# Turning keys and queries of all half batches on TensorE instead of by transposing loads

## The chip, the cores and the metric

The kernel runs on one core of a Trainium2 chip. The metric is the device time of one execution in microseconds (us); the median of three runs of the kernel before is 398.96 us (396.92 to 400.0). A core has five engines that work side by side, each through its own queue in program order: TensorE (PE in the profile; PEld is its loading of weights), VectorE (DVE), ScalarE (ACT), GpSimd (POOL) and SyncE (SP). In this kernel SP and POOL also issue the DMA transfers. TensorE writes to PSUM, a small memory of eight banks, from which DVE or ACT copy results into SBUF.

## What is computed

Attention with a sliding window and a few global tokens, then an MLP whose activation is h * cos(h):

```python
# q, k, v: (8 batches, 8 heads, 576 tokens, 64)    global_idx: 8 tokens
scores = scale * np.matmul(q, k.transpose(0, 1, 3, 2))
mask = np.abs(pos[:, None] - pos[None, :]) <= 32
mask = mask | is_global[:, None] | is_global[None, :]
attn = softmax(np.where(mask, scores, -1e9))
attn_out = np.matmul(attn, v)
x = attn_out.transpose(0, 2, 1, 3).reshape(4608, 512)
h = x @ w_in                    # (512, 2048)
out = (h * np.cos(h)) @ w_out   # (2048, 512)
```

Inputs and output are fp32; the kernel computes in fp16 with fp32 sums.

## The kernel before

**Tiles.** The work of attention is cut into 32 pairs of heads (`pr`, four to a batch) and two pairs make a half batch (`s`, 16 of them). A pair's 576 queries are cut into 11 blocks of 56; each block has, with the 8 global tokens, 64 query columns for each of the two heads, and 120 keys of the window with the 8 global keys as 128 rows. So a pair needs keys with the head dimension on partitions (`kw`, 128 x 11 x 128) and queries likewise (`qb`, 128 x 11 x 2 x 64), four buffers of each.

**How keys and queries get turned.** There are two ways in the kernel, and the constant `HY` parts them (lines 410 to 430):

- Half batches below HY = 4: `load_qk` (L256) brings k and q straight from the input into SBUF as fp16, with tokens on partitions, by two DMAs of POOL's queue. `turned` (L401) transposes a pair on TensorE: 8 rows x 2 heads = 16 transposes for keys (86 x 64 each) and 16 for queries (78 x 64) into a PSUM tile `t`. For keys ACT copies `t` into `kw` (L414); for queries ACT copies the first head and DVE the second into `qb` (L427).
- Half batches from 4 on: `cast_half` (L244) has POOL's queue cast k and q into an fp16 scratch in DRAM (`k16`, `q16`, L253), `turn_half` (L263) has SP's queue bring them back with two transposing loads into `kT` and `qT` (L265, L266), and DVE copies from there into `kw` (L417) and `qb` (L430).

Values of every half batch are cast to a scratch `v16` (L249) and loaded from there by SP's queue as overlapping windows (`load_v`, L296; the rows of the global tokens by `load_vg`, L314).

**One pair.** `scores` (L432): 11 matmuls in three groups into PSUM tiles `st`, the exponential on ACT (L442), the product with the mask on DVE (L443). `values` (L446): 22 matmuls into `pv`, then on DVE the sums and the division (L457 to L463). `turn_x` (L467): six transposes into `tx`, copied by DVE into `xT`; after a batch's last pair POOL copies its global rows (L483).

**The MLP.** `mlp_in` (one block: four matmuls of 128x512 at L491, the cosine on ACT at L494, the product on DVE at L495) and `mlp_out` (one block: four matmuls at L505; after four blocks a copy of `o` by ACT or DVE and a store by SP's queue).

**The order.** It is written out by hand and each engine keeps it. Strings give the order: `FRONT` for the first pairs, `THIRD` for s=2, and `ORDER` for each step s=3 to 15 of the loop at L684. In a step, `sa` and `sz` are the scores of the half's two pairs (three groups each), `pa` and `pz` the values, `xa` and `xz` the turns of x, `n` a sum of squares on ACT, `1` a block of `mlp_in`, `2` a block of `mlp_out` (in the early steps fewer are let through, `outs_by`), `G` the issue of casts (`casts`, L660), and `kc qc kd qd` the preparation of keys and queries of the two pairs of the next half:

```python
ORDER = "sa0 sa1 sa2 2 2 2 sz0 2 sz1 sz2 pa 1 1 2 xa pz G 1 1 2 xz n 1 1 2 kc qc 1 kd qd 2 1"
```

At the end of step s come `turn_half(s + 2)` and the value loads of half s + 2, all on SP's queue, which also holds the stores of the output. After the loop a tail does what is left of the MLP.

**PSUM.** The tiles `st`, `tx` and (after FRONT) `t` share three slots with the tag "s"; `ph` of `mlp_in` has two with the tag "h", `po` one with the tag "o", and `pv` its own.

Of the kernel before, what the change touches and what calls it, by code (L numbers as in the profile page):

```python
# [24 lines left out]
W = 120  # L25
BP = 6
KL = 32
HY = 4
RW = 8
KPAD = 4  # L30
KP = KPAD + S // RW + 10
# [23 lines left out]
def dview(ap, offset, *dims):  # L55

    return bass.AP(ap.tensor, ap.offset + offset, [list(d) for d in dims])
# [134 lines left out]
def kernel(  # L192
# [51 lines left out]
    def cast_half(s, which):  # L244

        base = s * 4 * S * D
        for x in which:
            if x == "v":
                nc.gpsimd.dma_start(v16[s * 4 * S : (s + 1) * 4 * S].rearrange("(n r) d -> n (r d)", r=16),  # L249
                                    dview(v, base, (16 * D, 4 * S // 16), (1, 16 * D)))  # L250
            else:
                src, dst = {"k": (k, k16), "q": (q, q16)}[x]
                nc.gpsimd.dma_start(dst[s].rearrange("t (h d) -> t h d", h=4),  # L253
                                    dview(src, base, (D, S), (S * D, 4), (1, D)))

    def load_qk(s):  # L256

        base = s * 4 * S * D
        for src, dst in ((k, kn[s % 2][KPAD : KPAD + S // RW]), (q, qn[s % 2][0 : S // RW])):
            nc.gpsimd.dma_start(dst.rearrange("x h r d -> x h (r d)"),  # L260
                                dview(src, base, (RW * D, S // RW), (S * D, 4), (1, RW * D)))

    def turn_half(s):  # L263

        nc.sync.dma_start(kT[s % 2][:, :, KL : KL + S], k16[s], transpose=True)  # L265
        nc.sync.dma_start(qT[s % 2][:, :, 0:S], q16[s], transpose=True)  # L266
# [19 lines left out]
    def gather(src, dst, half):  # L286
        rows = src.rearrange("b h s d -> (b h s) d")
        for h in range(2):
            nc.gpsimd.indirect_dma_start(
                out=dst[:, half, h], out_offset=None, in_=rows,  # L290
                in_offset=bass.IndirectOffsetOnAxis(ap=gidx_rows[:, 0:1], axis=0),
                element_offset=(half * 32 + h) * S * D)
# [80 lines left out]
    def build_globals(half):  # L373
        for src, dst in ((kg32, kgT), (qg32, qgT)):
            g16 = work.tile([P, P], FP16, tag="g16")
            nc.scalar.copy(g16, src[:, half].rearrange("x h d -> x (h d)"))
            t = ps.tile([P, 16 * G], FP16, tag="s", bufs=3)
            nc.tensor.transpose(t, g16, ident16)
            nc.scalar.copy(dst[:, 16 * half : 16 * half + 16], t.rearrange("x (n g) -> x n g", g=G))
        nc.scalar.copy(vg16[:, half], vg32[:, half])  # L380
# [20 lines left out]
    def turned(src, pr, n):  # L401

        t = ps.tile([P, RW, n], FP16, tag="h" if front[0] else "s", bufs=2 if front[0] else 3)
        h0 = 2 * (pr % 2)
        for r in range(RW):
            for h in range(2):
                nc.tensor.transpose(t[h * D : (h + 1) * D, r], src[:n, h0 + h, r], ident16[:n, :n])  # L407
        return t

    def local_k(pr):  # L410
        to = kw[pr % NK][:, :, G:]
        if pr < 2 * HY:
            t = turned(kn[pr // 2 % 2], pr, KP)
# [5 lines left out]
    def local_q(pr):  # L419
        if pr < 2 * HY:  # L420
            t = turned(qn[pr // 2 % 2], pr, QP)
        for h in range(2):
            hp = slice(h * D, (h + 1) * D)
            to = qb[pr % NK][hp, :, h, G:]
            if pr < 2 * HY:
                copy = nc.scalar.copy if h == 0 or pr < 2 else nc.vector.tensor_copy
                copy(view(to, (2 * C, NB), (RW, QB // RW), (1, RW)),  # L427
                     view(t[hp], (QB // RW, NB), (1, QB // RW), (QP, RW)))
            else:
                nc.vector.tensor_copy(to, view(qT[pr // 2 % 2][hp, pr % 2], (QB, NB), (1, QB)))  # L430
# [89 lines left out]
    def x_squares(s):  # L520

        sq = work.tile([P, 2 * BP * P], FP16, tag="sq", bufs=1)
        xn = xn_of.pop(s)
        nc.scalar.activation(sq, view(xn, (1, 2 * BP * P)), AF.Square,  # L524
                             accum_out=x_sq[:, s : s + 1])
# [47 lines left out]
    def one(n=1):  # L573
        for _ in range(n):

            if ins_q and ins_q[0][0] < ready[0] and ins_q[0][0] < outs_q[0][0] + 2:
                t, f = ins_q.pop(0)
                mlp_in(t, f)
                ready[1] = t * NF + f + 1

    def two(n=1):
        for _ in range(n):
            t, u = outs_q[0] if outs_q else (NTT, 0)

            need = min(t * NF + 4 * (u % 4) + 12, NTT * NF) if tail[0] else min(t * NF + 4 * (u % 4) + 7, (t + 1) * NF)
            if outs_q and need <= ready[1] and (tail[0] or NTT * NF - len(outs_q) < outs_by[0]):
                mlp_out(*outs_q.pop(0))
# [7 lines left out]
    with tc.manual_schedule():  # L595
# [48 lines left out]
        def load_values(pr):  # L644
            load_v(pr)
            load_vg(pr)
# [9 lines left out]
        def globals_kq(pr):  # L656
            globals_k(pr)
            globals_q(pr)

        def casts(s):  # L660

            nc.gpsimd.tensor_copy(gate, xn_of[s][0:1, 1, 0, 0:1])  # L662
            for n in range(4, 2 * B):
                if s == (n - 2 if n < 7 else n - 3):
                    cast_half(n, "vkq")
            if s == 4:
                for src, dst in ((k, kg32), (q, qg32), (v, vg32)):
                    gather(src, dst, 1)
# [15 lines left out]
        for s in range(2, B * NP // 2):  # L684
            if s == 2:
                nc.gpsimd.dma_start(w_out16, moe_w_out.rearrange("(c p) n -> p c n", p=P))
            outs_by[0] = 4 * (s - 2) if s < 5 else 8 * (s - 3)
            for pr in (2 * s + 2, 2 * s + 3):
                if 8 <= pr < B * NP:
                    globals_kq(pr)  # L690
            for step in (THIRD if s == 2 else ORDER).split():
                if step == "1":
                    one()
                elif step == "2":
                    two()
                elif step == "n":
                    x_squares(s - 1)
                elif step == "G":
                    casts(s)
                else:  # L700
                    f, pr = (STEPS | LOCAL)[step[0]], 2 * s + "azcd".index(step[1])
                    if pr < B * NP:
                        f(pr, *[int(x) for x in step[2:]])
            if s % 2 == 1:
                ready[0] = s // 2 + 1 + (s // 2 == B - 1)
            if s < B * NP // 2 - 2:
                turn_half(s + 2)
                load_values(2 * s + 4)
                load_values(2 * s + 5)
            if s == 5:  # L710
                build_globals(1)
# [49 lines left out]
```

## Time and profile before

| | |
|---|---|
| runs | 398.96, 400.0, 396.92 us |
| the profiled execution | span 395.4 us from the first to the last instruction; its time outside the span is not listed |
| PE busy | 328.3 us, 83% |
| DVE busy | 260.6 us, 66% |
| ACT busy | 238.8 us, 60% |
| POOL busy | 114.8 us, 29% |
| software DMA queue (POOL's) | 63952 packets, 18.75 MB, 48.4% of 16 engines |
| hardware DMA queue (SP's) | 124509 packets, 27.89 MB, 59.6% of 16 engines |
| chain that ended last | PE 67%, DMA 10%, DVE 8%, ACT 5% |
| L407 (transposes of half batches 0 to 3) | 256 instructions |
| L253 (casts of k and q, half batches 4 to 15) | 24 DMAs |
| L265, L266 (transposing loads) | 24 DMAs |

How to read it: "busy" is the sum of an engine's instructions; a matmul's listed duration holds its latency, and matmuls overlap, so PE's pace is read from the distance of their starts. In an answer of the timeline a line has start, duration, engine, line of the kernel and operation, and in brackets how long the engine had stood idle before it and what ended that. Windows give each engine's busy time in a stretch, the clock granted to TensorE (1.00 is full) and the share of the DMA engines' time that transfers took.

### The profile page before, as it was taken

The page shows a single profiled execution, that of the slowest core. Times are in us where ns is not written, and L with a number is a line of the kernel's source. Part 1 is how long each engine was busy: PE and PEld are TensorE (multiplying, and loading weights), DVE is VectorE, ACT ScalarE, POOL GpSimd, SP SyncE. Part 2 cuts the span into 40 slices and gives each one's busy share as a digit, 9 for nine tenths or more (in the row PEclk, how much of TensorE's full clock was granted, in tenths as well). Part 3 has the DMA queues.
Part 4 walks back from the last instruction along what each step waited for, and adds up shares of the span by engine and source line. Part 5 has one row for each costly group of instructions (what it writes and reads, how often), then busy time and mean ns, then how long its engine had stood idle before and what let it go on. Part 6 is the DMA issues. An engine that isn't in the chain of part 4 may idle for free.

```text
span 395.4 us, 7373 instructions
## 1 busy us (share of the span) xinstructions
PE 328.3 (83%) x2678; PEld 174.7 (44%) x2678; DVE 260.6 (66%) x600; ACT 238.8 (60%) x351; POOL 114.8 (29%) x250
## 2 busy tenths in 40 slices
PE   0272179576778889899999999999999979999993
PEld 0262164343434355455555555555555334444441
DVE  7744157555687768789788888888889354544300
ACT  1572066945575686677778678776777866244210
POOL 6573032504268275071443507223000100000000
PEclk9997558969999999999999999999999999999999
DMA  6989979999999999999999999999990000010121
GB/s 92 96 123 199 123 43 181 215 130 124 176 121 177 108 175 131 166 154 180 149 176 187 127 177 140 191 141 120 144 118 31 27 2 27 28 54 27 55 80 60
DMA packets 188504, 47.18 MB, mean 119 GB/s; under 512 B 177005, under 2 KB 183405, under 8 KB 188205
## 3 DMA queue, kind: packets, MB, share of 16 engines
q1 hardware_dynamic: 124509, 27.89, 59.6%
q0 software_dynamic: 63952, 18.75, 48.4%
q8 instruction: 23, 0.38, 0.5%
q14 instruction: 20, 0.16, 0.2%
HBM read 47.73 MB, written 21.23 MB: 174 GB/s over the span
## 4 chain that ended last, share of the span: by engine, by line
PE 67%; DMA 10%; DVE 8%; ACT 5%; issue 3%; SPq 3%; another core or an unknown queue 1%; POOL 0%; ACTq 0%; DVEq 0%
PE po L505 28%; PE ph L491 27%; DMA q<-in_q_dram 4%; PE st L440 4%; PE pv L452 4%; DMA vw<-vg 3%; DMA vw<-v 3%; DVE g L495 2%; PE tx L475 2%; SPq L308 2%; ACT cos L494 2%; DVE xn L463 1%; PE t L407 1%; ACT sq L524 1%
## 5 line engine op out<-in xcount | busy, mean ns | idle before, releaser
L491 PE MATMUL ph<-xT,w_in 128*128 128x512 f16 x576 | 142.8, 385 | 6.7 <-DVE g L495 5.9
L505 PE MATMUL po<-w_out,g 128*128 128x512 f16 x576 | 140.4, 380 | 5.0 <-DMA w_out<-in_moe_w_out_dram 3.6
L494 ACT ACTIVATE cos<-ph,pio 128x512 f16<-128x512 f32 x144 | 97.3, 686 | 77.2 <-PE ph L491 75.6
L495 DVE TENSOR_TENSOR g<-cos,ph 128x512 f16<-128x512 f16 x144 | 96.4, 685 | 55.0 <-ACT cos L494 52.7
L505 PEld LDWEIGHTS <-g 128*128 128x128 f16 x576 | 55.4, 98 | 67.7 <-issue 5.2
L491 PEld LDWEIGHTS <-w_in 128*128 128x128 f16 x576 | 54.1, 99 | 69.4 <-issue 13.1
L442 ACT ACTIVATE e<-st 128x512 f16<-128x512 f32 (+1 forms) x96 | 47.6, 561 | 14.3 <-PE st L440 9.3
L443 DVE TENSOR_TENSOR pm<-e,mask 128x512 f16<-128x512 f16 (+1 forms) x96 | 37.0, 405 | 23.8 <-ACT e L442 21.9
L662 POOL COPY gate<-xn 1x1 f16<-1x1 f16 x14 | 2.5, 182 | 143.3 <-DVE xn L463 143.3
L452 PE MATMUL pv<-vw,pm 128*64 128x65 f16 x704 | 20.6, 204 | 23.1 <-issue 10.3
L440 PE MATMUL st<-qb,kw 128*128 128x128 f16 x352 | 30.8, 238 | 4.2 <-ACT e L442 1.5
L440 PEld LDWEIGHTS <-kw 128*128 128x128 f16 x352 | 26.3, 108 | 14.2 <-POOL xT L483 2.9
L463 DVE TENSOR_TENSOR xn<-pv,r_all 128x768 f16<-128x768 f32 x32 | 30.6, 958 | 1.9
L452 PEld LDWEIGHTS <-pm 128*64 128x64 f16 x704 | 16.6, 117 | 27.3 <-issue 19.0
L253 POOL DMA_DIRECT2D q<-in_q_dram x12 | 27.6, 2304 | 0.0
L414 ACT COPY kw<-t 128x1320 f16<-128x1320 f16 x8 | 10.1, 1257 | 28.7 <-PE t L407 28.7
L483 POOL COPY xT<-xg 128x4 f16 x64 | 20.5, 320 | 22.0 <-DVE xT L478 18.6
L510 ACT COPY o<-po 128x512 f32<-128x512 f32 x18 | 10.5, 586 | 22.4 <-PE po L505 21.9
L524 ACT ACTIVATE sq<-xn 128x1536 f16<-128x1536 f16 x16 | 23.6, 1474 | 0.0
L430 DVE COPY qb<-qT 64x616 f16<-64x616 f16 x48 | 22.1, 460 | 0.3
L253 POOL DMA_DIRECT2D k<-in_k_dram x12 | 21.2, 1765 | 0.3 <-issue 0.3
L512 DVE COPY o<-po 128x512 f32<-128x512 f32 x18 | 12.3, 685 | 12.1 <-PE po L505 12.0
(106 smaller groups left out, 269.2 us busy)
## 6 DMA issues: line engine op xcount, KB each, us to landing
out_dram<-o SPq DMA_DIRECT2D x36, 256.0 KB
vw<-v SPq DMA_DIRECT2D x47, 165.0 KB
v<-in_v_dram POOLq DMA_DIRECT2D x16, 288.0 KB
k<-in_k_dram POOLq DMA_DIRECT2D x12, 288.0 KB
q<-in_q_dram POOLq DMA_DIRECT2D x12, 288.0 KB
vw<-v SPq DMA_DIRECT2D x16, 135.0 KB
w_in<-in_moe_w_in_dram POOLq DMA_DIRECT2D x4, 512.0 KB
w_out<-in_moe_w_out_dram POOLq DMA_DIRECT2D x1, 2048.0 KB
```

What stands on the lines that cost most here:

```text
L253: nc.gpsimd.dma_start(dst[s].rearrange("t (h d) -> t h d", h=4), dview(src, base, (D, S), (S * D, 4), (1, D)))
L430: nc.vector.tensor_copy(to, view(qT[pr // 2 % 2][hp, pr % 2], (QB, NB), (1, QB)))
L440: nc.tensor.matmul(st[:, j], kp[:, g0 + j], view(qp[:, g0 + j], (1, P)), start=True, stop=True)
L442: nc.scalar.activation(e[:, :n], st[:, :n], AF.Exp, scale=scale)
L443: nc.vector.tensor_tensor(view(pm[:, g0], (1, n * P)), view(e, (1, n * P)), view(mask[:, g0], (1, n * P)), ALU.mult)
L452: nc.tensor.matmul(pv[r0 : r0 + C, j // 6, c0 : c0 + 65], pm[:, j, h], vp[:, j, h], start=True, stop=True)
L463: nc.vector.tensor_tensor(view(xn, (384, 2), (D, 6), (1, D)), view(pv, (512, 2), (65, 6), (1, D)), view(rp, (6, 2), (1, 6), (0, D)), ALU.mult)
L491: nc.tensor.matmul(ph, w_in16[:, j, f * P : (f + 1) * P], xT[:, j, t * TT : (t + 1) * TT], start=(j == 0), stop=(j == NC - 1))
L494: nc.scalar.activation(cos, ph, AF.Sin, bias=pio2)
L495: nc.vector.tensor_tensor(g16[:, f], cos, ph, ALU.mult)
L505: nc.tensor.matmul(po, g16[:, f, s * P : (s + 1) * P], w_out16[:, f], start=(f == 0), stop=(f == NF - 1))
L524: nc.scalar.activation(sq, view(xn, (1, 2 * BP * P)), AF.Square, accum_out=x_sq[:, s : s + 1])
```

## The change

HY goes from 4 to 16, so every half batch takes the first of the two ways. `casts` issues `load_qk(n)` and the cast of v at step s = n - 2, where it had issued the casts of v, k and q at n - 2 for n below 7 and at n - 3 from there on. `turn_half` is not called any more.

```diff
-HY = 4
+HY = 16
...
             nc.gpsimd.tensor_copy(gate, xn_of[s][0:1, 1, 0, 0:1])
             for n in range(4, 2 * B):
-                if s == (n - 2 if n < 7 else n - 3):
-                    cast_half(n, "vkq")
+                if s == (n - 2 if n < max(7, HY) else n - 3):
+                    if n < HY:
+                        load_qk(n)
+                    cast_half(n, "v" if n < HY else "vkq")
...
             if s < B * NP // 2 - 2:
-                turn_half(s + 2)
+                if s + 2 >= HY:
+                    turn_half(s + 2)
                 load_values(2 * s + 4)
                 load_values(2 * s + 5)
```

The SBUF tiles `kn` and `qn` that `load_qk` fills have two buffers each: half n goes into the one that half n - 2 held, and that was turned in step n - 3.

## The prediction

> **What bounds the kernel now.** I read the slices of the page first, then windows cut at the steps of the loop over s, then TensorE's waits in the timeline, and last the stretch where the kernel already does what the change makes it do in every step.
>
> The slices (tenths of about 9.9 us each):
>
> ```profile
> PE   0272179576778889899999999999999979999993
> PEclk9997558969999999999999999999999999999999
> DMA  6989979999999999999999999999990000010121
> ```
>
> The DMA engines are full until slice 30, which invites the reading that they bound the kernel. They do so only where PE is not full as well. From about slice 17 to 31 PE is at 9 at full clock, and the next view says how full. One step of the loop starts where its first scores (L440) start; I cut windows of one step's length, one step after another, with busy times by engine:
>
> ```profile
> core 0: us, PE busy (x) PEld busy (x) DVE busy (x) ACT busy (x) POOL busy (x), PEclk, DMA share, GB/s
> ...
> 243.82:260.73 16.91, 16.91 (x143) 9.07 (x142) 14.49 (x34) 12.91 (x20) 6.81 (x16) 1.00 1.66 165
> 260.73:277.65 16.92, 16.92 (x144) 9.07 (x142) 14.50 (x34) 12.92 (x20) 3.27 (x15) 1.00 1.45 133
> 277.65:294.57 16.92, 16.92 (x144) 9.07 (x142) 14.59 (x34) 12.93 (x20) 0.18 (x1) 1.00 1.31 122
> ```
>
> Two things are to be seen. PE has no gap. And the step is the same 16.92 us whether the casts run (165 GB/s) or are over (122 GB/s): here the transfers cost nothing. The chain of waits gives the step as a sum of PE's own pace: 16 blocks of four 128x512 matmuls (L491, L505) at 0.864, 22 scores for 1.22 (0.61+0.22+0.39), 44 value products for 1.00, 12 turns of x for 0.68: 16.7 of the 16.92. So in steps s=8 to 15 whatever is added to PE's queue lengthens the kernel, and no transfer that is taken away shortens it.
>
> In steps s=3 to 7 PE does wait. Their first scores start at 74.98, 99.68, 118.22, 140.05, 157.00, and s=8's at 175.37, so they last 24.70, 18.54, 21.83, 16.95 and 18.37. Steps 3 and 4 have four blocks of L505 fewer (16.92 - 4 x 0.864 = 13.46). Against full pace they lose 11.2, 5.1, 4.9, 0.0 and 1.5: **22.7 us**, the most that could be won. The waits for DMA in PE's timeline:
>
> ```profile
> 79.32 1.49 PE L505 MATMUL po<-w_out,g 128*128 128x512 f16 x4 [3.57 <-DMA w_out<-in_moe_w_out_dram]
> ...
> 83.50 1.02 PE L452 MATMUL pv<-vw,pm 128*64 128x65 f16 x22 [1.52 <-DMA vw<-vg]
> ...
> 91.61 0.76 PE L452 MATMUL pv<-vw,pm 128*64 128x65 f16 x22 [3.03 <-DMA vw<-v]
> ...
> 129.55 0.19 PE L452 MATMUL pv<-vw,pm 128*64 128x65 f16 x1 [0.88 <-issue]
> ...
> 166.56 0.76 PE L452 MATMUL pv<-vw,pm 128*64 128x65 f16 x22 [1.19 <-DMA vw<-vg]
> ```
>
> The first is w_out, queued at 60.28 ahead of every transfer that the change touches: it stays. The others, 6.6 us, are values that arrive late because they share the engines and SP's queue with casts and transposing loads. The rest of the 22.7 is latency of ACT, DVE and POOL (waits for xn, g, o, xT) and the half clock of 76 to 88 us.
>
> **What is removed.** Twelve half batches (4 to 15) lose two casts on POOL and two transposing loads on SP. POOL's starts at 69.26, 69.79, 70.87, 71.94 show 0.53 for the v cast, 1.08 for k and 1.07 for q; the direct loads that replace them start 0.74 apart (38.53, 39.27): POOL wins 0.7 us a step. That is worth something where PE waits for POOL: 0.95 before the scores at 99.68. On SP the transposing loads take 1.3 to 4.4 us of issue each and stand ahead of the value loads. DVE loses per step two key copies of 0.53 and four query copies of 0.46: 2.9 us; DVE has 2.4 us idle in a full step, so this gives PE nothing.
>
> Of the 6.6 us, 0 to 6.6 vanish; k and q still come (the same 288 KB each in the issue table), so contention remains, but without the scratch's second trip. I take 5, as SP's queue is relieved too. With POOL's 0.95 the gain is **6 us**, from 0 to 8.
>
> **What is added on PE.** 64 transposes of L407 a step (two pairs, k and q, 8 rows x 2 heads), in steps s=3 to 14. The front shows pair 6, at full clock:
>
> ```profile
> 68.64 0.50 PE L407 MATMUL t<-ident,kn 86*64 86x86 f16 x16
> 68.97 0.45 PE L407 MATMUL t<-ident,qn 78*64 78x78 f16 x16
> 69.36 0.51 PE L475 MATMUL tx<-ident,xn 128*128 128x128 f16 x6
> 69.34 1.25 ACT L414 COPY kw<-t 128x1320 f16<-128x1320 f16 x1
> 70.48 0.67 ACT L427 COPY qb<-t 64x616 f16<-64x616 f16 x1
> 71.18 0.80 DVE L427 COPY qb<-t 64x616 f16<-64x616 f16 x1 [1.02 <-ACT qb L427]
> ```
>
> By starts, keys take 0.33 and queries 0.39: 0.72 a pair, 1.44 a step, **17.3 us** in 12 steps. Under half clock (54.80 to 55.47) queries alone take 0.67; at full clock I take 0.72. Nothing hides this in s=8 to 14: 7 x 1.44 = 10.1 us are certain even if steps 3 to 7 hid all of theirs.
>
> **What is added behind it.** Each tile t takes one of the three "s" slots of PSUM, shared with the scores. ACT gains 1.25 + 0.67 per pair, 3.84 a step: 12.92 becomes 16.8. DVE gains 0.80 per pair, and this copy waits for ACT's (idle 1.02 above). Queued behind the waiting copy on DVE are the product g of L495 and the masks of the next scores; PE waits for the slot. I walk one step with these rows, 0 being the start of kc, after "n 1 1 2". PE: kc to 0.33, qc 0.71, "1" 1.57, kd 1.90, qd 2.29 (it needs kc's slot, which ACT frees at about 1.8), "2" 3.15, "1" 4.0, then sa0, sa1, sa2 at 4.0, 4.2, 4.45. ACT starts kc's copy at 0.5 and, at its rows' start-to-start pace, qc at 1.65, the cosine at 2.2, kd 2.8, qd 3.95, done at 4.6. DVE then copies until 5.45. sa0 needs qc's slot (DVE done near 3.15: free), sa1 kd's (4.05: free), sa2 needs qd's: it waits from 4.45 to about 5.5. **A stall of 1.0 us**, 12.5 us in 12 steps. After it ACT has a copy of o, a cosine, a table load of 1.28 and three exponentials, while PE has 2.6 us of "2 2 2" before it needs sa0's slot again: just enough. No stall of this kind is in the full steps of before; bounds: 0 (ACT ahead by 1 us) to 2.5 (all the ACT work of 3.84 less the 1.44 of new PE work). I take 1.0, nearest to the walk.
>
> The Trainium skill, TensorEngine Tiling (Array Packing), section Performance Considerations, says that packing speeds TensorE but not the emptying of PSUM, and advises both ScalarE and VectorE for it. The trace agrees: 0.72 us of transposes against 2.7 us of copies in a row. By the rule read strictly the copies would set the pace; that is the second rival.
>
> **Sum.** +17.3 + 12.5 - 6 = +24 us on the profiled execution (span 395.4; its own time is not listed, the runs shown lie 1.5 to 4.6 above the span, the median 3.6). I take a little off, as gaps of latency in steps 3 to 5 will swallow some of the transposes there (three steps of 1.44, half of them: 2): 398.96 + 22 = **421 us**.
>
> **Rivals.**
> 1. No stall: ACT keeps ahead and sa2 finds its slot. For it: ACT has 4.0 us idle in a full step. Against: the walk. 17.3 - 6 - 2: 408 us, up to 413 with half the gain. Chance 0.25.
> 2. ACT and the PSUM slots set the pace: the stall is near 2.5 and passes on to the next scores. 17.3 + 30 - 6: 440 us. For it: 16.8 us of ACT in a step of 18.4. Chance 0.14.
> 3. Faster: the full DMA engines are what holds steps 3 to 7, and all 22.7 us there were theirs. With no stall 17.3 - 22.7 = -5.4: 393 us. It decides once more than 17.3 us comes back; only 6.6 are named DMA waits, and w_out's 3.57 stays. Chance 0.04.
> 4. Late values: from half 7 on the v cast is issued one step later and behind k and q, and SP's value loads wait for it, with the stores of o behind them. At s=2 the q cast landed 17.34 us after its issue; value loads have about a step and a third (22 us) less SP's own 8 to 12. If it decides it costs some 1 us a step: 430 us. Against: less traffic than then. Chance 0.07.
> 5. The clock falls. In the windows it is 1.00 in every full step though 12 turns of x stand in it; after PE's idle at 76 us it was 0.50. If the stalls dropped it for 4 us a step, 24 us more: 445 us. Chance 0.04. The Trainium skill, TensorE: Matmul & The Clock Gate, Part 4, says that transposes do not count as work for the clock gate; the trace shows 32 of them from 68.64 on under a granted clock of 1.00, so I give that rule no more than this.
> That the change does nothing is excluded: the transposes stand in PE's queue.
>
> **Numbers.** Forecast 421 us, chance 0.46. The range 407 to 438 takes in the bounds of the stall up to 2.3 us a step and of the gain (rival 1 to its lower end); it leaves out the faster case, rival 5, and the upper half of rival 2, 0.15 to 0.2 in all. About 1% (4 us) is what a measurement can tell from no change: faster 0.04; same 0.03 (rival 1 with all bounds of the gain); slower 0.93.
>
> **What would show it.** Right: full steps of 18.4 to 19.5 us, 64 L407 per step at 0.72 a pair, waits of L440 for DVE or ACT qb near 1 us, ACT at 16.8 a step, DMA share well below 1.4, the waits for vw at 83 to 92 and 166 gone, the tail from the end of s=15 unchanged (84 us). Wrong: steps of 18.4 without such waits (rival 1), PE waits for vw in full steps (4), PEclk below 9 (5), or steps 3 to 7 shorter by more than 17 us (3).

## The result, and the profile after

The changed kernel takes **430.39 us** (median of four runs, 428.56 to 431.73) against 398.72 us (396.92 to 400.0): ratio 1.083, 95% interval 1.078 to 1.088. It is 31.7 us slower. The profiled execution has a span of 429.7 us, 34.3 more than the one of before.

The slices of the page after (about 10.7 us each):

```profile
PE   1270479387849989999999999999999987998994
PEclk9986569669997999999999999999999999999998
DMA  5999969998978595959799789969680000010021
```

The DMA row has become thinner, as the change meant: the hardware queue moves 20.81 MB instead of 27.89, the software queue 17872 packets instead of 63952. The kernel is slower all the same, so the full DMA row of before did not bound it. PE is as full as before, for longer, and shows a new dip to 4 in the twelfth slice (118 to 129 us) with a lower clock in the one behind it.

Windows of one step of the loop over s (us, then busy time by engine, clock, DMA share, GB/s):

```profile
core 0: us, PE busy (x) PEld busy (x) DVE busy (x) ACT busy (x) POOL busy (x), PEclk, DMA share, GB/s
...
170.60:190.10 19.50, 18.69 (x207) 10.26 (x206) 13.53 (x29) 16.16 (x24) 5.10 (x18) 1.00 0.85 110
...
268.40:287.90 19.50, 18.69 (x208) 10.26 (x207) 13.54 (x29) 16.17 (x24) 3.58 (x10) 1.00 0.91 110
```

A full step lasts 19.5 us where it lasted 16.92, and PE now has 0.8 us without work in each. The timeline of the end of one step shows whose:

```profile
264.24 0.50 PE L407 MATMUL t<-ident,kn 86*64 86x86 f16 x16
264.57 0.45 PE L407 MATMUL t<-ident,qn 78*64 78x78 f16 x16
...
264.78 1.26 ACT L414 COPY kw<-t 128x1320 f16<-128x1320 f16 x1 [0.61 <-PE t L407]
...
265.92 0.50 PE L407 MATMUL t<-ident,kn 86*64 86x86 f16 x16
265.94 0.67 ACT L427 COPY qb<-t 64x616 f16<-64x616 f16 x1
266.25 0.45 PE L407 MATMUL t<-ident,qn 78*64 78x78 f16 x16
...
267.08 1.25 ACT L414 COPY kw<-t 128x1320 f16<-128x1320 f16 x1
...
268.22 0.67 ACT L427 COPY qb<-t 64x616 f16<-64x616 f16 x1
...
268.93 0.80 DVE L427 COPY qb<-t 64x616 f16<-64x616 f16 x1 [0.77 <-ACT qb L427]
...
269.79 0.33 PE L440 MATMUL st<-qb,kw 128*128 128x128 f16 x3 [0.81 <-DVE qb L427]
```

PE has finished qd's transposes at about 266.6, ACT empties the two last tiles until 268.9, DVE the last half until 269.73, and at 269.79 PE gets the slot for sa2. The bracket of the last line is the wait that the walk in the prediction placed.

Where the 34.3 us lie, by the starts of the steps (us):

| step | 3 | 4 | 5 | 6 | 7 | 8 to 14 | from s=15 to the end |
|---|---|---|---|---|---|---|---|
| before | 24.70 | 18.54 | 21.83 | 16.95 | 18.37 | 118.4 | 101.6 |
| after | 27.53 | 20.45 | 28.99 | 18.59 | 19.52 | 136.8 | 102.8 |
| difference | 2.8 | 1.9 | 7.2 | 1.6 | 1.2 | 18.4 | 1.2 |

Steps 3 to 7, where the prediction expected something back, lose 14.7 us. Half of that is one hole, at the border of steps 4 and 5:

```profile
121.27 0.30 PE L407 MATMUL t<-ident,qn 78*64 78x78 f16 x5 [0.47 <-issue]
...
122.04 0.20 PE L407 MATMUL t<-ident,qn 78*64 78x78 f16 x1 [0.48 <-issue]
...
125.72 1.26 ACT L414 COPY kw<-t 128x1320 f16<-128x1320 f16 x1 [3.01 <-remote]
...
127.04 0.58 PE L440 MATMUL st<-qb,kw 128*128 128x128 f16 x4 [3.61 <-issue]
...
128.89 0.48 PE L440 MATMUL st<-qb,kw 128*128 128x128 f16 x3 [1.27 <-DVE qb L427]
129.16 4.97 PE L505 MATMUL po<-w_out,g 128*128 128x512 f16 x12
```

PE stops in the middle of a row of transposes, ACT before a copy whose input is there; neither bracket names an engine ("issue" and "remote" are waits that the profile cannot put down to one). The twelve matmuls behind it take 4.97 us; the same group takes 2.75 in the full step, and the granted clock from 127 to 133 us was 0.50.

The waits for DMA in steps 3 to 7, to be set beside the five shown of before:

```profile
80.03 1.87 PE L505 MATMUL po<-w_out,g 128*128 128x512 f16 x4 [4.20 <-DMA w_out<-in_moe_w_out_dram]
...
86.98 0.23 PE L452 MATMUL pv<-vw,pm 128*64 128x65 f16 x1 [3.91 <-DMA vw<-vg]
87.67 0.81 PE L452 MATMUL pv<-vw,pm 128*64 128x65 f16 x21 [0.45 <-DMA vw<-vg]
```

The waits for values in step 3 have moved to the first pair but are as long: 4.36 us against 1.52 + 3.03. Those of steps 5 and 7 are gone. The early steps vary from one execution to the next: step 3 of the changed kernel lasts 27.5 us here and 25.7 in a second profile (experiment 5), so their figures are good to about 2 us.

### The profile page after: what moved, and what is told of

It is laid out like the page before. It is cut to its first block, busy times and chain, and to the rows that moved or that the text cites. A ratio compares the mean times of both kernels' runs of the same rounds, so it can differ in the third digit from the quotient of the medians.

```text
span 429.7 us, 8882 instructions
## 1 busy us (share of the span) xinstructions
PE 351.1 (82%) x3446; PEld 189.3 (44%) x3446; DVE 248.0 (58%) x552; ACT 278.4 (65%) x399; POOL 88.7 (21%) x250
## 3 DMA queue, kind: packets, MB, share of 16 engines
q1 hardware_dynamic: 96093, 20.81, 43.5%
q0 software_dynamic: 17872, 18.76, 27.7%
## 4 chain that ended last, share of the span: by engine, by line
PE 61%; DVE 11%; ACT 11%; issue 5%; DMA 5%; SPq 4%; another core or an unknown queue 2%; ACTq 0%
PE po L505 27%; PE ph L491 23%; DMA vw<-vg 5%; ACT qb L427 4%; DVE qb L427 4%; DVE g L495 3%; PE pv L452 3%; PE st L440 3%; PE t L407 2%; PE tx L475 2%; ACT kw L414 2%; SPq L316 2%; ACT cos L494 2%; SPq L308 1%
## 5 line engine op out<-in xcount | busy, mean ns | idle before, releaser
L505 PE MATMUL po<-w_out,g 128*128 128x512 f16 x576 | 143.6, 386 | 4.6 <-DMA w_out<-in_moe_w_out_dram 4.2
L491 PEld LDWEIGHTS <-w_in 128*128 128x128 f16 x576 | 53.1, 99 | 65.6 <-issue 11.1
L414 ACT COPY kw<-t 128x1320 f16<-128x1320 f16 x32 | 40.2, 1255 | 37.9 <-PE t L407 34.8
L427 DVE COPY qb<-t 64x616 f16<-64x616 f16 x30 | 24.1, 803 | 39.9 <-ACT qb L427 39.9
L440 PE MATMUL st<-qb,kw 128*128 128x128 f16 x352 | 32.9, 239 | 15.7 <-DVE qb L427 9.6
L427 ACT COPY qb<-t 64x616 f16<-64x616 f16 x34 | 22.7, 668 | 6.1 <-remote 5.0
L407 PE MATMUL t<-ident,qn 78*64 78x78 f16 x512 | 16.1, 208 | 9.5 <-ACT qb L427 4.6
L407 PE MATMUL t<-ident,kn 86*64 86x86 f16 x512 | 17.3, 218 | 7.7 <-DVE vw L618 7.7
L407 PEld LDWEIGHTS <-kn 86*64 86x64 f16 x512 | 13.2, 121 | 18.8 <-issue 11.2
```

Source lines behind the costliest of these rows:

```text
L414: nc.scalar.copy(view(to, (P, NB), (RW, W // RW), (1, RW)), view(t, (QB // RW, NB), (1, W // RW), (KP, RW)))
L427: copy(view(to, (2 * C, NB), (RW, QB // RW), (1, RW)), view(t[hp], (QB // RW, NB), (1, QB // RW), (QP, RW)))
L440: nc.tensor.matmul(st[:, j], kp[:, g0 + j], view(qp[:, g0 + j], (1, P)), start=True, stop=True)
L491: nc.tensor.matmul(ph, w_in16[:, j, f * P : (f + 1) * P], xT[:, j, t * TT : (t + 1) * TT], start=(j == 0), stop=(j == NC - 1))
L505: nc.tensor.matmul(po, g16[:, f, s * P : (s + 1) * P], w_out16[:, f], start=(f == 0), stop=(f == NF - 1))
```

## The experiments

Each run was timed beside the kernel before on the same chip: 395.16 us for the first four, 396.85 for the next four, 396.20 for the last four. "s=3 to 7" is the time of those five steps in the profile (100.4 in the kernel before, 115.1 in the changed one), "full step" one of s=8 to 14.

**1. Transposes alone.** The kernel before (HY = 4), with `turned` called for the later half batches too and its result left unused:

```diff
         else:
+            turned(kn[pr // 2 % 2], pr, KP)
             nc.vector.tensor_copy(to, view(kT[pr // 2 % 2][:, pr % 2], (QB, NB), (1, W)))
...
-        if pr < 2 * HY:
-            t = turned(qn[pr // 2 % 2], pr, QP)
+        t = turned(qn[pr // 2 % 2], pr, QP)
```

> The kernel before with the 64 transposes of L407 added to each of the steps s=3 to 14, on keys and queries that lie in SBUF already; their results are copied by nobody, and kw and qb still come from the transposing loads, as before. Theory (PE is full, every transpose lengthens the step by its own pace of 1.44 us, and nothing else of the change costs on PE): a full step of 18.4 us, 17 us more than before, 414 to 416 us. Rival (the transposes fall into gaps and the cost of the change is the copies behind them): 399 to 402 us.

Measured: 408.85 us, 13.7 more than before (ratio 1.037, 1.033 to 1.041). A full step:

```profile
249.14:267.69 18.55, 18.55 (x208) 10.23 (x207) 14.53 (x34) 12.91 (x19) 6.00 (x12) 1.00 1.42 149
```

So 1.63 us a step for the 64 transposes, 0.19 more than their starts in the front gave. ACT and DVE are as in the kernel before. But s=3 to 7 last 100.0 us in the profile, no longer than without the transposes: PE's idle time there (the five steps less PE's busy time) falls from 18.7 to 12.4 us, and the clock in step 3 was higher (0.93 in the mean against 0.86). Not each of them took its transposes in: step 6, which had no gap, grows from 16.95 to 19.49 us. The seven full steps account for 11.4 of the 13.7 us, so the five early ones together cost between nothing (by the profile) and 2.3 us (by the times). The theory holds for full steps, the rival, nearly, for the early ones.

**2. The turns spread over the step.** One string of the changed kernel:

```diff
-ORDER = "sa0 sa1 sa2 2 2 2 sz0 2 sz1 sz2 pa 1 1 2 xa pz G 1 1 2 xz n 1 1 2 kc qc 1 kd qd 2 1"
+ORDER = "sa0 sa1 sa2 2 2 2 sz0 2 sz1 sz2 pa 1 1 2 xa pz G kc qc 1 1 2 xz n 1 1 2 kd qd 1 2 1"
```

> The changed kernel with one string changed: the first pair's turns (kc qc) stand after G, the second pair's (kd qd) where the first pair's stood, so that ACT and DVE have time between the two. Theory (1 us of each full step is PE's wait at sa2 for the PSUM slot that qd's copies hold): the wait for DVE qb L427 goes, a full step falls from 19.5 to 18.5 us, 418 to 420 us. Rival (ACT's 16 us of work a step sets the pace wherever the copies stand): 19.5 us a step, 429 to 432 us.

Measured: 411.18 us (ratio 1.044, 1.039 to 1.049), that is 16 us above the kernel before instead of 32. The full step:

```profile
251.43:270.08 18.65, 18.49 (x208) 10.28 (x206) 13.63 (x30) 16.22 (x24) 3.58 (x10) 1.00 0.89 115
```

ACT has the same 16.2 us of work, the wait for DVE qb L427 is gone from full steps, and the step falls by 0.87 us to within 0.1 of experiment 1. ACT's load does not set the pace; where the copies stand does. The time is 8 us below the forecast. Some 3.5 of these are the chip, on which the kernel before takes 395.16 us and not 398.72; the rest goes with the hole, which did not appear: s=3 to 7 last 102.4 us.

**3. Both heads copied by DVE.**

```diff
-            copy = nc.scalar.copy if h == 0 or pr < 2 else nc.vector.tensor_copy
+            copy = nc.scalar.copy if pr < 2 or (h == 0 and pr < 8) else nc.vector.tensor_copy
```

> The changed kernel with both heads of the queries copied by DVE (half batches 4 to 15), none by ACT. Theory (the slot of qd waits for ACT's chain kc, qc, cosine, kd, qd and then DVE): by the same walk DVE ends at about 4.65 instead of 5.4 where PE arrives at 4.45, so the wait falls from 0.9 to about 0.2 us, a step of 18.8 us, 421 to 423 us. Rival (load of ACT): each step loses what ACT loses, 1.3 us, 18.2 us a step, 414 us. Rival (no slot wait): 430 us.

Measured: 413.78 us (ratio 1.047, 1.043 to 1.051). A full step takes 18.75 us where the walk said 18.8 and the rival 18.2. The run parts the two less sharply than planned, since ACT's work fell by 0.9 us a step (16.17 to 15.26) and the step by 0.76; it is experiment 2, with all of ACT's work in a step of 18.65, that rules the rival out. Here too the whole is 8 us below the forecast, for the same two reasons (s=3 to 7: 104.5, no hole).

**4. The scratch put back beside the new way.**

```diff
-                    cast_half(n, "v" if n < HY else "vkq")
+                    cast_half(n, "vkq")
...
-                if s + 2 >= HY:
-                    turn_half(s + 2)
+                turn_half(s + 2)
```

> The changed kernel with the casts of k and q to the scratch and the transposing loads put back beside the new way (nobody reads what they bring). Theory A (as predicted: the scratch's traffic and its place in POOL's and SP's queues cost 6 us in steps 3 to 7): 436 us or more. Theory B (the waits of steps 3 to 7 were those of w_out and of latency, and taking the scratch away gave back 1 to 2 us at s=7 alone): 430 to 433 us.

Measured: 442.45 us in the median of four runs, of which one took 490.93 and the others 441.62 to 443.04 (ratio of these three 1.119, 1.114 to 1.123), some 15 us above the changed kernel. Values come late here, in step 5 and in every second full step (23.71, 24.50 and 22.28 us instead of 19.5):

```profile
135.44 1.13 PE L452 MATMUL pv<-vw,pm 128*64 128x65 f16 x22 [4.34 <-DMA vw<-vg]
...
261.23 0.19 PE L452 MATMUL pv<-vw,pm 128*64 128x65 f16 x1 [2.38 <-DMA vw<-vg]
262.14 0.51 PE L452 MATMUL pv<-vw,pm 128*64 128x65 f16 x21 [0.72 <-DMA vw<-vg]
```

At first sight steps 3 to 7 lose almost nothing: they last 115.8 us, 0.7 more than in the changed kernel. But that kernel has the hole there, and this one does not: step 4 lasts 18.90 us. Against the changed order without the hole (experiment 9, 107.9 us) steps 3 to 7 lose 7.9 us, and the seven full steps 12.2. Theory B falls. Theory A had its 6 us in the early steps, and a loss of about that size is there, but it had none in full steps. This kernel moves more than either of the two (54.4 MB) and casts v a step later than the kernel before, whose full steps show no such wait. So it does not price the scratch of the kernel before; it shows how little room the value loads have once the later cast meets that traffic.

**5. The changed kernel again.**

> The changed kernel once more. In its first profile step s=5 lasted 28.99 us, 9.5 us more than a full step, with ACT idle for 3.0 us at 122.7 for a cause outside the engines and TensorE at half clock behind it. Theory 1 (that is an event of one execution): step 5 lasts 21 to 24 us here. Theory 2 (it belongs to the kernel): step 5 again lasts near 29 us. Either way full steps of 19.5 us with a wait for DVE qb L427 of 0.8 us in each.

Measured: 429.43 us (ratio 1.081, 1.072 to 1.089). Step 5 lasts 28.55 us, ACT again waits 2.92 us for "remote" and PE 3.52 for "issue" at the same place. The hole belongs to the kernel and not to one execution.

**6. Every transpose twice.**

```diff
         for h in range(2):
-            nc.tensor.transpose(t[h * D : (h + 1) * D, r], src[:n, h0 + h, r], ident16[:n, :n])
+            for _ in range(2 if pr > 7 else 1):
+                nc.tensor.transpose(t[h * D : (h + 1) * D, r], src[:n, h0 + h, r], ident16[:n, :n])
```

> The changed kernel with every transpose of half batches 4 to 15 issued twice into the same place, so TensorE has another 1.44 us in each of the steps s=3 to 14 and ACT and DVE the same copies. Theory (the end of the turns is set by the chain of copies that begins after the first tile of keys, and TensorE's other transposes lie inside the time that it would wait at sa2 anyway): a full step grows by some 0.4 us, to 19.9 to 20.1 us, and the wait at sa2 goes; 5 us in all. Rival (TensorE's own work counts in full, the wait stays): 21.0 us a step, 17 us in all.

Measured: 434.48 us (ratio 1.091, 1.083 to 1.100), 5 us above the changed kernel on the same chip. The full step:

```profile
252.30:272.13 19.83, 19.83 (x271) 11.46 (x270) 13.54 (x30) 16.28 (x24) 5.10 (x18) 1.00 0.93 110
```

64 more transposes add 0.31 us, a little less than the theory's 0.4, and PE has no gap left: the doubled work went into the wait. So in the changed kernel the end of a step is set by the row of copies, and PE's time after the first tile is paid for only beyond that row.

**7. The casts of v at the old place.**

```diff
+                    load_qk(n)
+                if s == (n - 2 if n < 7 else n - 3):
+                    cast_half(n, "v")
-                    if n < HY:
-                        load_qk(n)
-                    cast_half(n, "v" if n < HY else "vkq")
```

> The changed kernel with the casts of v at the step where the kernel before has them (n - 3 from half 7 on); the direct loads of k and q stay at n - 2. Theory (the later cast costs nothing, the value loads still come in time in full steps): within 2 us of the changed kernel. Rival (late values, SP's loads wait for the cast): 3 to 8 us faster, out of steps 5 to 7.

Measured: 427.51 us (ratio 1.071, 1.063 to 1.080), 1.9 us below the changed kernel on the same chip with intervals that overlap. Full steps are 19.52 us. The later cast costs at most that; steps 4 and 5 came out at 44.3 us instead of 48.9, with a smaller hole.

**8. HY = 8 with the turns spread.** Experiment 2 with `HY = 8`.

> The kernel with the turns spread as before and HY = 8: half batches 4 to 7 are turned on TensorE (steps 3 to 6), 8 to 15 come by transposing loads. Theory (steps 3 to 7 have gaps that take in the transposes, as they did where transposes alone were added, and only full steps pay): 0 to 3 us slower than the kernel before; full steps of 16.92 us from s=8 on. Rival (each turned half batch costs the same): 4 x 1.7 = 7 us slower. If taking the scratch away helps early: 1 to 4 us faster.

Measured: 409.9 us (ratio 1.030, 1.022 to 1.037): 13 us slower, a miss for theory and rival alike. In this order the full steps without any turn on TensorE last 18.20 us:

```profile
213.59 1.89 PE L491 MATMUL ph<-xT,w_in 128*128 128x512 f16 x8 [1.12 <-DVE g L495]
```

`kc qc` after G now puts DVE's copies from `kT` and `qT` ahead of the products that free the slots of `ph`. An order that helps one way of turning hurts the other, so this run tells nothing of half batches 4 to 7; experiment 12 does.

**9. The gathers spread.** During the hole POOL is issuing six gathers of global rows, all at s=4. Here two go at each of s=2, 3, 4:

```diff
-            if s == 4:
-                for src, dst in ((k, kg32), (q, qg32), (v, vg32)):
+            for at, src, dst in ((2, k, kg32), (3, q, qg32), (4, v, vg32)):
+                if s == at:
                     gather(src, dst, 1)
```

> The changed kernel with POOL's six gathers of the global rows of the second half of the batches, all issued at s=4, issued two at a time at s=2, 3 and 4. In three profiles of the changed order TensorE and ACT stand still for 3 to 5 us while those six are being issued (from 118.5 to 125.8 in the first). Theory (the hole in steps 4 and 5 comes with the gathers): steps 4 and 5 together fall from 49 to about 42 us, 7 us in all, 421 to 424 us; full steps stay at 19.5. Rival (it comes from elsewhere): steps 4 and 5 stay at 49 us, 429 to 431 us.

Measured: 422.51 us (ratio 1.065, 1.057 to 1.072). Steps 4 and 5 take 41.9 us together instead of 49.4 and 48.9: the hole is gone, and in the steps it was worth 7 to 7.5 us. By the whole time, each against the kernel before on its own chip, the move gave 5.4 to 6.3 us (26.3 us slower instead of 31.7 and 32.6).

**10. The same in the kernel before.**

> The kernel before with the same move of the gathers. If the gathers hold up the engines there too, part of the 4.9 us that step 5 loses comes back: 2 to 4 us faster than the kernel before. If not: within 1 us of it, or slower by 1 us as the gathers then stand ahead of casts in POOL's queue at s=2.

Measured: 395.21 us against 396.20 (ratio 0.998, 0.994 to 1.001): no difference that can be told. In its profile step 5 is 2.9 us shorter and step 4 is 1.5 longer.

**11. Turns and gathers spread.**

> The changed kernel with the turns spread (kc qc after G) and the gathers spread. Full steps of 18.65 us as in the run with the turns spread alone; that run showed no hole, so moving the gathers should give at most 1 us: 10 to 16 us slower than the kernel before. What is left would be TensorE's own share, 1.6 us in each full step.

Measured: 413.09 us (ratio 1.043, 1.037 to 1.050), 17 us above the kernel before, just outside the 10 to 16 forecast, and no better than experiment 2.

**12. HY = 8, order as it was.** The changed kernel with `HY = 8` alone.

> The changed kernel with HY = 8 and the order as it was: half batches 4 to 7 turned on TensorE (steps 3 to 6), 8 to 15 by transposing loads. Theory (full steps pay 2.6 us each for their own turns and nothing else; the hole of steps 4 and 5 belongs to the early steps): full steps of 16.92 us again from s=8 on, 11 to 14 us slower than the kernel before, all of it lost in steps 3 to 7. Rival (the cost is even over the turned half batches, 2.6 us for each of 4): 10 us slower with steps 4 and 5 as in the kernel before.

Measured: 400.61 us (ratio 1.014, 1.006 to 1.021), 4.4 us slower, with an interval from 2.3 to 8.5 us. The full steps are as in the kernel before:

```profile
242.00:258.92 16.92, 16.92 (x144) 9.08 (x143) 14.49 (x34) 12.92 (x20) 7.32 (x19) 1.00 1.62 159
258.92:275.84 16.92, 16.92 (x144) 9.07 (x143) 14.49 (x34) 12.92 (x20) 4.91 (x9) 1.00 1.54 162
```

Steps 4 and 5 take 41.9 us, without the hole, though the six gathers stand at s=4 as in the changed kernel and are issued at the same time (116.8 to 124.1). Up to G of step 5, which comes after that, the two kernels do the same work in the same order: only the constant differs. So both expectations were too high, the theory's by the hole. It is also the cleanest split of the cost: four turned half batches in the early steps cost 4 us; the eight behind them, and the hole that comes with them, cost the rest.

No version here with more half batches turned on TensorE beats the kernel before.

## Why the prediction was right, and where it was not

The direction and the range held; 421 us was forecast and 430.4 came. By parts: for the seven full steps the sum had 7 x (1.44 + 1.04) = 17.4 us, and 18.4 came; for steps 3 to 7 it had 12.4 - 6 - 2 = 4.4, and 14.7 came, half of it in a hole that nobody foresaw; for the rest it had nothing, and 1.2 came. So the account of the full steps was right and that of the early steps was not. That 430.4 still lies in the range is partly luck: the room above 421 was kept for a longer stall, which did not come, and the hole used it.

- **"PE has no gap", so whatever is added to its queue lengthens the kernel.** Right: with the transposes alone (experiment 1) each full step grew by what was added, and the thinner DMA row gave full steps nothing.
- **17.3 us for the transposes.** The size per step was a little low (1.63 against 1.44), and the sum let nearly all twelve steps pay. Alone the transposes cost 13.7 us, 11.4 of it in the seven full steps; the early steps hid most or all of theirs, where the sum allowed 2 us for that.
- **A stall of 1.0 us at sa2.** Right in place, cause and size: 0.81 us in the bracket, 0.97 between the full steps of experiment 1 and of the changed kernel, 0.87 won by moving the turns apart, 18.75 against 18.8 in experiment 3, and the 0.3 us of experiment 6. Rival 1 (no stall) and rival 2 (ACT sets the pace) fall: ACT carries 16.2 us (16.8 were forecast) in a step of 18.65 without holding it up.
- **The gain of 6 us.** This is the step that failed, with the next. Of the 6.6 us of waits that it started from, 0.88 is put down to "issue" and to no DMA; the named waits for values were 5.74 us before and are 4.36 after, all in step 3. The chain of waits (start, us, what) shows what happened there, before and then after:

```profile
70.87 17.34 DMA q<-in_q_dram
...
88.23 1.52 SPq L266
...
89.86 1.74 DMA vw<-v
```

```profile
72.87 8.18 SPq L316
...
81.10 6.52 DMA vw<-vg
```

Before, the value load that PE waited 3.03 us for did stand behind the q cast and q's transposing load, as the prediction said, and that wait is gone. In its place PE waits for the rows of the global tokens, which SP takes 8.2 us to issue and which land 6.5 us later. Which of the transfers then under way holds them up (w_out, or the direct loads of k and q) is not shown. The 0.95 us of PE waiting for POOL went into other waits. In experiment 9, without the hole, s=3 to 7 last 107.9 us, 7.5 more than in the kernel before and 7.9 more than with the transposes alone (experiment 1). Of these 7.9 us, 5.0 are idle time of PE (17.4 against 12.4), 4.0 of them waits for the copies of `kw` and `qb`, a part of the stall that the sum did have; 2.9 are longer busy time, with a mean clock of 0.75 in step 3 against 0.93.
- **The hole of 7 to 7.5 us at steps 4 and 5** was in no term and no rival. The clock is at half for a few microseconds behind it, as rival 5 feared after a stall; in full steps, with their 0.8 us gap, the clock stays at 1.00. What causes the hole is open. It is there in the first profile and in those of experiments 5 and 6, weaker in 7 and 8, and gone in experiments 2, 3, 4, 9, 11 and 12. The gathers alone are not the cause, nor is the order of work up to there, since 12 has both as in the changed kernel. That PE and ACT had run out of fetched instructions would fit brackets without an engine. The trace does not tell: the queue of kind "instruction" moves one block between 117 and 127 us in the changed kernel, which has the hole, and in experiments 9 and 12, which have not. No run was made for it.
- **Rival 3, faster,** falls: steps 3 to 7 became longer, not shorter.
- **Rival 4, late values.** Not in full steps of the changed kernel: none waits for vw. Experiment 7 leaves at most 2 us for the later cast. Experiment 4 shows that it becomes real when the scratch's traffic is added.

Put together for the profiled execution: 7 x 1.63 = 11.4 us of transposes and 7 x 0.97 = 6.8 us of slot wait in full steps, 7.5 us for the hole, 7.2 us of other loss in steps 3 to 7, 1.2 us from s=15 on: 34.1 of 34.3. The 7.2 us are the least sure of these: in experiment 9 4.0 us are waits for the copies, the rest is in part the clock of step 3, and the early steps vary by about 2 us. Of the 22.7 us that the prediction saw lost there before, 9.3 are named waits for DMA, 3.57 of them for w_out; the half clock lay from 79.7 to 86.6 us, and not from 76 to 88. Latency and clock were not shortened by removing transfers, and the new copies added waits of their own.

The rule of the Trainium skill that the prediction weighed against the stall (TensorEngine Tiling (Array Packing), Performance Considerations: packing does not speed the emptying of PSUM) agrees with experiment 6, where twice the transposes cost 0.31 us a step and the copies behind them set its end. Its page's advice to use both ScalarE and VectorE did not help in this form: ACT and DVE emptied the tile of queries one after the other, and with DVE alone for it (experiment 3) a step was quicker by 0.76 us. As to the rule from TensorE: Matmul & The Clock Gate, Part 4, that transposes do not count as work for the clock gate: full steps with 128 transposes (experiment 6) ran at a granted clock of 1.00, so no run here shows a loss by it.

## What to carry to other kernels

Cut the trace at the steps of the loop before deciding what bounds it: a DMA row at 9 beside a PE row without gaps meant here that the transfers were covered, and work moved to TensorE cost its full time there (1.63 us a step). When a tile in PSUM is added to a shared ring of slots, walk the ring by hand with the copy durations; the place of the tiles in the order was worth 0.9 us a step here, as much as the choice of engine. And count on no gain from removed traffic unless the trace shows which transfer the wait was for.

## What the runs showed that was not expected

Transposes to the two halves of the columns ran side by side: 16 of them, 86 columns each, took 0.33 us, half of what one after the other would take at the pace of the scores (0.61 us for 11 of 128 columns, 0.43 ns a column, so 0.59). In the trace they start two at a time, 3 to 4 ns apart. Put into the early steps alone, where PE had gaps, they cost 0 to 2.3 us. And PE and ACT stood still for 3 to 5 us with nothing in the profile to name for it, at the same place in repeated runs, and lost that stop when POOL's gathers were moved, or when nothing up to that place was changed but a constant that acts later.
